# Row sums moved to the end of a PV batch, the range check moved ahead of the next inverse, and loads spread behind every second mask

## The chip, the cores and the metric

The kernel runs on one core of a Trainium2 chip. The metric is the device time of one execution in microseconds; lower is better. The same kernel is up to 2.8 us slower on one chip than on another (the kernel before: medians of 609.1 to 611.9 us), so an experiment is always told as its ratio to the kernel before on the same chip.

## The reference, cut to what matters

Two independent attention layers, A and B, with sliding-window causal masks:

```python
B, S, D = 1, 2048, 1024;  H = 32; Dh = 32; W = 256
qkv = (x @ wqkv).reshape(B, S, 3, H, Dh).transpose(2, 0, 3, 1, 4)
scores = einsum("bhqd,bhkd->bhqk", q, k) * Dh ** -0.5
mask = (i - j >= 0) & (i - j < 256)
p = softmax(where(mask, scores, -1e9))
return einsum("bhqk,bhkd->bhqd", p, v).transpose(...).reshape(B, S, D) @ wo
```

## The kernel before

The program is a list of 152 sessions. A session computes one set of score tiles on TensorE (line 511), takes exp of them on ScalarE (L521), and cuts the window out with masks on GpSimd (L532, L545). Behind some masks GpSimd clears one column of a buffer (a guard for the load that follows), and SyncE issues that load. Every second session, as a rule, ends with one or two PVs on TensorE: probabilities times values, and probabilities times ones, which gives the row sums of the softmax. The PVs of one session are called a batch. The rest of a session is filled with pieces of the projections, as "whole" 128x512 matmuls or, in sessions with a PV, as four strips of 32 columns.

```python
edgep = tile_pool(name="edge", bufs=2)          # the buffers of `both`
...
while len(pieces.get(free, [])) >= min(2 if key[0] == "x" else 4, <masks of that session>):
    free += 1                                   # the session that issues a load
...
def diag(a, g, j, i):
    nc.gpsimd.affine_select(out=diags[(g, p)]..., in_=pt..., ...)
    load_piece(now)                             # a load behind every mask, as long as there is one

def edge(g, p):                                 # VectorE: two masked parts added, so that
    both = edgep.tile([P, 4, 2, P], BF16)       # one matmul with ones can sum both (L559)
    ... tensor_tensor(out=both..., in0=dg..., in1=pts..., op=ALU.add)

def pv(g, p):
    moves = [...values..., ...sums over pt...]
    sums = edges.pop((g, p)) if p else dg
    moves += [(i, 0, 2 * P, P, sums[:, :, i, :]) for i in range(2)]     # the sums over `both`
    for x, (h, j, o, w_, src) in enumerate(moves): ...matmul...          # L592
    # norm, on VectorE: reciprocal (L605), two shuffles, multiply (L612),
    # and after every second multiply the range check of the inverses (L615):
    scalar_tensor_tensor(out=top, in0=inverses..., scalar=IN_RANGE, in1=top, xor, or)
...
    while due and due[0][0] <= now:             # end of a session: one or two PVs
        finish_norm(1)
        pv(pg, pk)
...
finish_norm()
certify[0](top)                                 # reduce the range checks
emit(END + 10, 2 * NS_MM * CT)                  # two pieces of projection meanwhile
certify[1](ps_proj)                             # verdict: TensorE sums it over partitions
```

`both` has two buffers, and a buffer comes free when the row sums over it have been computed on TensorE. All loads go through the one queue of SyncE, in the order in which they are issued. And when the program is built, the scheduler takes an x for landed three sessions after the one that issues its last piece (`arrival[key] = free + 3`), and from then on it may place projections that read it.

## Time and profile before

| | |
|---|---|
| time | 609.8 us |
| span of the profiled execution | 608.7 us |
| TensorE busy | 96% |
| VectorE, ScalarE, GpSimd busy | 67%, 68%, 59% |

The prediction below shows the lines on TensorE. The groups of the page for the engines around it are read for their last two columns: the time for which the engine sat idle just before this group, and what ended most of that.

```profile
L521 ACT ACTIVATE pt<-st 128x1024 bf16<-128x1024 f32 x304 | 302.2, 1026 | 107.9 <-PE st L511 55.1
L532 POOL TENSOR_SCALAR_AFFINE_SELECT diag<-pt 128x256 bf16<-128x256 bf16 x512 | 211.2, 438 | 195.2 <-ACT pt L521 181.7
L559 DVE TENSOR_TENSOR both<-diag,pt 128x512 bf16<-128x512 bf16 (+1 forms) x256 | 123.7, 525 | 55.5 <-PE acc L592 27.4
```

Each of them waits for another engine for a large share of the run.

### The profile page before, as it was taken

How to read it: one execution, taken by the hardware profiler on the slowest of the kernel's cores; microseconds unless marked ns; L12 is line 12 of the kernel's file. 1: busy time of each engine (PE TensorE's matmuls, PEld its weight loads, DVE VectorE, ACT ScalarE, POOL GpSimd, SP SyncE). 2: the span in 40 equal slices, each digit the busy share in tenths (PEclk: the TensorE clock that was granted, in tenths of full speed). 3: DMA queues.
4: the chain of work that ended last, by engine and by line, in shares of the span. 5: the costliest groups of instructions: out<-in, count | busy, mean ns of one | idle time of the engine just before them, and what ended most of it. 6: DMA issues, size and time to landing. Idle time of an engine off the chain costs nothing.

```text
span 608.7 us, 32535 instructions
## 1 busy us (share of the span) xinstructions
PE 586.9 (96%) x14364; PEld 363.4 (60%) x14439; DVE 409.8 (67%) x1144; ACT 412.1 (68%) x523; POOL 361.1 (59%) x918
## 2 busy tenths in 40 slices
PE   9999999999999999999999999999999999999996
PEld 6566566657655666665665766675555665555443
DVE  1388786877887867866587766766868777767200
ACT  4577867777678778786567766777667677765332
POOL 0567666767777676766466666666666666664000
PEclk9999999999999999999999999999999999999998
DMA  9714110111034102454211100112030030114222
GB/s 238 177 53 128 38 38 5 38 37 39 4 65 80 40 3 51 98 93 105 52 38 37 38 4 4 45 32 73 2 86 24 18 95 11 56 55 133 71 78 65
DMA packets 86820, 35.73 MB, mean 59 GB/s; under 512 B 65552, under 2 KB 86160, under 8 KB 86672
## 3 DMA queue, kind: packets, MB, share of 16 engines
q1 hardware_dynamic: 85632, 33.31, 22.3%
q8 instruction: 115, 1.88, 1.3%
q10 hardware_dynamic: 1040, 0.26, 0.2%
q14 instruction: 33, 0.27, 0.2%
HBM read 17.83 MB, written 8.39 MB: 43 GB/s over the span
## 4 chain that ended last, share of the span: by engine, by line
PE 65%; issue 1%; ACT 0%; DVE 0%; ACTq 0%
PE pp L197 31%; PE pp L201 19%; PE acc L592 8%; PE st L511 6%; ACT pt L521 0%; ACT osb L220 0%; DVE unsafe_i L888 0%; PE pp L887 0%; ACTq L220 0%; ACT kT L220 0%
## 5 line engine op out<-in xcount | busy, mean ns | idle before, releaser
L521 ACT ACTIVATE pt<-st 128x1024 bf16<-128x1024 f32 x304 | 302.2, 1026 | 107.9 <-PE st L511 55.1
L532 POOL TENSOR_SCALAR_AFFINE_SELECT diag<-pt 128x256 bf16<-128x256 bf16 x512 | 211.2, 438 | 195.2 <-ACT pt L521 181.7
L559 DVE TENSOR_TENSOR both<-diag,pt 128x512 bf16<-128x512 bf16 (+1 forms) x256 | 123.7, 525 | 55.5 <-PE acc L592 27.4
L545 POOL TENSOR_SCALAR_AFFINE_SELECT pt<-pt 128x512 bf16<-128x512 bf16 (+1 forms) x256 | 155.6, 626 | 0.0
L197 PE MATMUL pp<-xT,wqk 128*128 128x512 bf16 (+1 forms) x581 | 135.8, 373 | 6.5 <-issue 5.2
L605 DVE RECIPROCAL rinv<-acc 128x128 f32<-128x128 f32 x128 | 121.6, 950 | 27.2 <-PE acc L592 25.4
L201 PE MATMUL pp<-xT,wqk 128*32 128x512 bf16 x1608 | 96.9, 379 | 0.0
L197 PEld LDWEIGHTS <-wqk 128*128 128x128 bf16 x638 | 59.1, 98 | 62.3 <-issue 0.3
L197 PE MATMUL pp<-wo_sb,oT 128*128 128x512 bf16 (+1 forms) x349 | 77.7, 374 | 2.2 <-issue 1.6
L511 PEld LDWEIGHTS <-kT 32*64 32x64 bf16 x3904 | 41.7, 103 | 57.6 <-issue 56.3
L197 PE MATMUL pp<-wv,xT 128*128 128x256 bf16 x587 | 71.0, 273 | 0.3 <-issue 0.3
L511 PE MATMUL st<-qT,kT 32*64 32x64 bf16 (+4 forms) x3904 | 66.7, 236 | 1.9 <-issue 0.9
L610 DVE STREAM_SHUFFLE wide<-rinv 128x128 f32<-128x128 f32 x256 | 64.3, 296 | 0.0
L220 ACT CAST osb<-pp 128x512 bf16<-128x512 f32 (+1 forms) x61 | 35.4, 581 | 42.1 <-PE pp L197 28.7
L197 PEld LDWEIGHTS <-xT 128*128 128x128 bf16 x587 | 55.5, 98 | 11.9 <-issue 0.4
L201 PEld LDWEIGHTS <-wqk 128*32 128x32 bf16 x1608 | 42.1, 97 | 31.4 <-issue 0.2
L197 PEld LDWEIGHTS <-oT 128*128 128x128 bf16 x367 | 34.7, 98 | 39.5 <-issue 0.2
L201 PE MATMUL pp<-wv,xT 128*32 128x256 bf16 x1748 | 55.7, 273 | 2.4 <-issue 2.1
L612 DVE TENSOR_TENSOR oT<-acc,wide 128x256 bf16<-128x256 f32 x128 | 54.4, 425 | 4.4
L201 PEld LDWEIGHTS <-xT 128*32 128x32 bf16 x1748 | 46.2, 97 | 7.8 <-issue 4.1
L592 PE MATMUL acc<-pt,vt 128*32 128x128 bf16 (+2 forms) x1792 | 48.8, 223 | 0.0
L592 PEld LDWEIGHTS <-vt 128*32 128x32 bf16 x2816 | 43.5, 96 | 7.7 <-issue 0.4
(47 smaller groups left out, 385.7 us busy)
## 6 DMA issues: line engine op xcount, KB each, us to landing
out_dram<-osb SPq DMA_DIRECT2D x63, 128.0 KB, 1.9
wqk<-in_B_wqkv_dram SPq DMA_DIRECT2D x32, 128.0 KB, 2.8
wqk<-in_A_wqkv_dram SPq DMA_DIRECT2D x24, 128.0 KB, 3.0
wo_sb<-in_A_wo_dram SPq DMA_DIRECT2D x16, 128.0 KB, 2.7
wv<-in_B_wqkv_dram SPq DMA_DIRECT2D x16, 128.0 KB, 3.6
wo_sb<-in_B_wo_dram SPq DMA_DIRECT2D x16, 128.0 KB, 2.3
oT<-in_A_x_dram SPq DMA_DIRECT2D x4, 256.0 KB, 5.1
wv<-in_A_wqkv_dram SPq DMA_DIRECT2D x2, 512.0 KB, 5.7
```

The lines of the kernel that those rows point to most:

```text
L197: nc.tensor.matmul(out[:, lo:hi], lhsT=lhsT, rhs=rhs, start=start, stop=stop, skip_group_check=True)
L201: nc.tensor.matmul(out[c:c + 32, lo:hi], lhsT=lhsT[:, c:c + 32], rhs=rhs, start=start, stop=stop, tile_position=(0, c), skip_group_check=True)
L220: nc.scalar.copy(out=out, in_=in_)
L511: nc.tensor.matmul(scores[c * HALF:(c + 1) * HALF, r, a * HALF:(a + w_) * HALF], lhsT=kT[rows, keys], rhs=qT[rows, q:q + w_ * HALF], start ...
L521: nc.scalar.activation(out=pt[:, lo:lo + 2, :n * HALF], in_=scores[:, lo:lo + 2, :n * HALF], func=ACT.Exp, bias=-SHIFT, scale=cfg.scale)
L532: nc.gpsimd.affine_select(out=diags[(g, p)][:, :, h, lo:lo + HALF], in_=pt[:, :, a * HALF:(a + 1) * HALF], pattern=[[0, 4], [1, HALF]], co ...
L545: nc.gpsimd.affine_select(out=blk, in_=blk, pattern=[[0, 4], [-1, w_ * HALF]], compare_op=ALU.is_gt, fill=0.0, base=-HALF * (us[a][2] - 3) ...
L559: nc.vector.tensor_tensor(out=both[:, :, h, o:o + w_], in0=dg[:, :, h, o:o + w_], in1=pts[t][:, :, a:a + w_], op=ALU.add)
L592: nc.tensor.matmul(acc[32 * r:32 * r + 32, o:o + w_], lhsT=lhsT, rhs=src[:, r, :], start=(x == 0), stop=(x == len(moves) - 1), tile_positi ...
L605: nc.vector.reciprocal(out=inverses[0][:, turn % 2, :], in_=acc[:, 2 * P:3 * P])
L610: nc.vector.stream_shuffle(out=wide[:, h * P:(h + 1) * P], in_=inverses[0][:, turn % 2, :], mask=[16 * h] * 32)
L612: nc.vector.tensor_tensor(out=oTs[(pi, k)][:, t, (p % 2) * 256:(p % 2 + 1) * 256], in0=acc[:, 0:256], in1=wide[:], op=ALU.mult)
```

## The change

Its intent: the row sums over `both` need VectorE's additions, so they go last in a session's batch, to give VectorE time. The range check stood between a norm and the next additions, so it goes ahead of the next inverse. And the loads' guards delay GpSimd's masks, so they are spread.

```diff
-            while len(pieces.get(free, [])) >= min(2 if key[0] == "x" else 4, <masks of the session>):
+            while len(pieces.get(free, [])) >= min(3, (calls_of(free) + 1) // 2):
...
-            load_piece(now)
+            if calls.pop():                    # calls = [False, True] * 8
+                load_piece(now)
...
-        for x, (h, j, o, w_, src) in enumerate(moves):
+        def move(x): ...the same four matmuls...
+        for x in range(len(moves) - 2):
+            move(x)
+        return lambda: finish_pv(g, p, acc, [lambda x=x: move(x) for x in (-2, -1)])
...
             if turn % 2 == 0:
+                check_range()
                 inverses[0] = normp.tile([P, 2, P], F32, name="rinv")
...
-            if turn % 2:
-                nc.vector.scalar_tensor_tensor(... range check ...)
...
+        tails = []
         while due and due[0][0] <= now:
-            finish_norm(1)
-            pv(pg, pk)
+            finish_norm(0 if tails else 1)
+            tails.append(pv(pg, pk))
+        for f in tails:
+            f()
...
     finish_norm()
+    check_range()
     certify[0](top)
```

(The same lines recur for the second kind of mask and for the PVs after the last session.)

The first pair of lines holds the cap on the loads of one session. It falls from four to three for the weights, but for x it rises from two to three.

## The prediction

> **What bounds the kernel now.** I read the page from the top: shares first, then the chain that ended last.
>
> ```profile
> PE 586.9 (96%) x14364; PEld 363.4 (60%) x14439; DVE 409.8 (67%) x1144; ACT 412.1 (68%) x523; POOL 361.1 (59%) x918
> ...
> PE 65%; issue 1%; ACT 0%; DVE 0%; ACTq 0%
> PE pp L197 31%; PE pp L201 19%; PE acc L592 8%; PE st L511 6%; ACT pt L521 0%; ACT osb L220 0%; DVE unsafe_i L888 0%; PE pp L887 0%; ACTq L220 0%; ACT kT L220 0%
> ```
>
> Every other engine is idle a third of the time, and the chain is all TensorE. So only what makes TensorE run fewer columns, change shape less often, or stand still can change the time. Next I made a ledger of TensorE. The built program has 14,438 matmuls in its fast path. Starts of whole 128x512 matmuls are 216 ns apart in the trace; I charged 216 ns per 512 columns, a quarter of it for one of four column strips (128*32), an eighth for a score tile (32*64): 549 us in all. A session (152 of them: scores, exp, masks, sometimes one or two PVs, then filler projections) changes the array's shape twice. The gap that the trace shows beyond the streaming, quartile of each kind: scores to whole 146 ns, scores to PV 134, strips to scores 103, whole to scores 93. With 78, 74, 74 and 78 of them that is 36 us. Together some 586 us. The last matmul starts at 602.8 us, the first at 1.3 us; so 15 to 16 us are left, of which some 5 are the start (waiting for the first rows of x, cold clock). The remaining 10 or 11 us are stalls of TensorE in the steady state: the most that this change could win (1.7%).
>
> The waits by engine say where they are not:
>
> ```profile
> PE pp L201 <- issue: 2.1, 4, 0.9
> PE acc L592 <- DVE both L559: 0.5, 2, 0.3
> PEld L511 <- issue: 56.3, 153, 0.6
> PEld L201 <- issue: 4.7, 9, 1.2
> PEld L592 <- issue: 2.7, 10, 0.4
> ```
>
> The 56.3 us at L511 are the shape changes, once a session. What a semaphore causes looks small (0.5 us), because a wait that begins under a modelled matmul end isn't counted. So I went to the timeline. The worst PV batch:
>
> ```profile
> 82.72 0.56 DVE L615 SCALAR_TENSOR_TENSOR top<-rinv,top 128x256 int32<-128x256 int32 x1
> ...
> 83.20 2.27 DVE L559 TENSOR_TENSOR both<-diag,pt 128x512 bf16<-128x512 bf16 x4
> ...
> 83.88 0.24 PE L592 MATMUL acc<-both,ones 128*32 128x128 bf16 x4 [0.18 <-DVE both L559]
> ...
> 84.42 0.24 PE L592 MATMUL acc<-both,ones 128*32 128x128 bf16 x4 [0.30 <-DVE both L559]
> ...
> 85.19 0.57 PE L592 MATMUL acc<-both,ones 128*32 128x128 bf16 x8
> 85.40 0.94 DVE L605 RECIPROCAL rinv<-acc 128x128 f32<-128x128 f32 x1
> ```
>
> VectorE does the range check (0.56 us), then four edge additions; TensorE meets the row sums over `both` before they are there, four times. Against an unhindered batch this one lost 1.39 us. Measured so, seven batches (ending at 38, 78, 86, 125, 172, 258 and 439 us) lost 2.9 us: the first kind of stall. The second kind has no semaphore:
>
> ```profile
> 204.24 0.70 PEld L201 LDWEIGHTS <-xT 128*32 128x32 bf16 x26
> 204.29 0.93 PE L201 MATMUL pp<-wv,xT 128*32 128x256 bf16 x25
> ...
> 206.17 1.16 PE L201 MATMUL pp<-wv,xT 128*32 128x256 bf16 x35 [0.95 <-issue]
> 206.17 0.88 PEld L201 LDWEIGHTS <-xT 128*32 128x32 bf16 x34 [1.23 <-issue]
> ...
> q8 instruction: 115, 1.88, 1.3%
> ```
>
> It stops in mid-chain, where no data can be missing. Counting weight loads, these stops fall at the same place modulo 256 TensorE instructions (weight loads 4064, 5088, 5344 and on), and the 16 KB packet of the instruction queue for each had begun about 2.35 us before TensorE went on. They are instruction fetches that come too late, about 7.4 us in the whole run.
>
> **What the Trainium skill says.** "TensorEngine Tiling (Array Packing)", Key Properties: changing the tiling mode drains TensorE. The trace agrees: 93 to 146 ns each. "TensorE: Matmul & The Clock Gate", Back-to-back issue gap: a warm matmul takes N/2.4 + 2.5 ns; 216 ns for 512 columns is what the trace shows. "Runtime: NRT & Kernel Launch", Instruction fetch mechanics: instructions come in 16 KiB blocks of 256, fetched one ahead, and the cost is "mostly hidden". The trace agrees on size (115 packets, 1.88 MB) but not on hidden[...]. "Perfetto Trace Analysis", Tensor Engine Instruction: matmul ends are estimated by the profiler; hence I went by starts.
>
> **The change, part by part.**
>
> Row sums at the end. The two `both` moves of each PV (8 matmuls, 0.11 us) go behind all else of the batch. No matmul is added: acc matmuls are 4,928 in both programs. Of the batches, about 51 hold two PVs. There the sums of the first PV now come after the other moves of the second, some 0.45 us later than before; those of the second only 0.11 us later. In the batch above the waits at 83.88 and 84.42 (0.18 + 0.30 in the view, 0.8 us against the unhindered pace) would be covered, and the last additions (83.20 + 2.27 = 85.47) still come late. In the other six only the very last addition was late, by 0.1 to 0.4 us; 0.11 us of each is won. That alone is 0.45 + 6 x 0.11, about 1.1 us. The price: in a two-PV batch the first reciprocal starts 0.5 us later; its acc buffer and its `both` buffer come free as much later. VectorE is 67% busy, so mostly this is absorbed.
>
> The range check. 64 of 0.41 to 0.58 us before and after; none is removed. It leaves the place between a norm and the next edge additions, and stands ahead of the next even reciprocal. In the built VectorE stream the order norm, check, additions stood 41 times (check directly ahead of additions); after the change that is nowhere, and 33 checks stand directly behind additions, where VectorE would wait for acc anyway (27.4 + 25.4 us of idle are put down to PE acc). Twelve stand behind an evacuation and 19 between two norms, where they delay the following additions as before. So about half of the seven late batches get their additions 0.4 to 0.56 us earlier: another 0.9 us, and I count 2.0 us of 2.9 for both parts.
>
> The loads. 144 guard memsets of 0.1 us remain; they stand behind every second mask, three a session at most instead of four. In load sessions a mask comes 0.1 to 0.2 us earlier, on an engine that waits for exp (181.7 us) rather than bounds. TensorE never waits for a DMA in the steady state. I give it 0.3 us. It does shift arrivals and so what the scheduler puts where: 27 projection steps change from strips to whole form (162 TensorE rows fewer, same columns), the 6.2 us session 80 is spread over later sessions, and the second half of the last weights arrives so late that the last two PVs stand back to back. The columns are the same, and so are the shape changes within one each, so the 586 us of the ledger stay.
>
> The fetches. Since the stream is shifted, the blocks of 256 are cut elsewhere. With the durations of the ledger, 23 of 111 blocks last under 3.35 us before, lacking 12.5 us in sum, of which 7.4 were really lost. After: 25 of 110, lacking 15.5. In proportion that is 9.2 us, 1.8 more. As a third of the short blocks escaped (their packet came early), I take 1.0 us.
>
> Sum: 609.8 - 2.0 - 0.3 + 1.0 = 608.5 us.
>
> **The rivals.** First, the waits only move: later row sums delay the first norm by 0.5 us, hence the next edge additions (their two buffers wait for these same row sums), and the next batch meets them late. For it: in the batches at 78, 125 and 172 us VectorE ran without a pause from the norm to the additions. Against it: those began behind an evacuation, not behind acc. It would leave 2.9 us of stalls as they are, or add one: about 610 to 611. Second, fetch decides: the recut stream stalls the full 1.8 us or more, or with luck 2 less; 607 to 611. Third, all goes well: batches wait for nothing, mask stream and loads run smoother, fewer strips ease the fetch: 5 us off, 604 to 605. Fourth, a load lands late and a projection waits on its DMA: several us at once, 613 or more. Against it: loads take 2 to 4 us to land, and the scheduler allows two or three sessions of 3.6 us.
>
> **Range and chances.** Most weight lies on a change under 0.7%. Winning 2% means 12.2 us, more than all steady stalls; losing 2% needs a new wait of 12 us, which only the fourth rival could make. I predict 608.5 us, 8 in 10 between 604.5 and 611.5; faster by over 2% 0.02, within 2% 0.955, slower 0.025.
>
> **What would show it.** TensorE busy stays within 1% of 586.9 us and the shares of the chain as they are. In PV batches the `both` matmuls stand last, eight or sixteen in a row, and stalls ahead of them sum to about 1 us. L615's successor stands ahead of reciprocals, mostly in former idle time before them. Stalls without a releaser remain at about 8 to 9 us, each behind a 16 KB packet. I am wrong if waits on VectorE's additions stay near 2.9 us, if fetch stalls fall, or if a DMA appears among the things that TensorE waits for.

## The result, and the profile after

The changed kernel took 619.2 us (619.0 to 620.5, four runs) against 609.8 us (609.7 to 610.2, four runs). The ratio is 1.0158, with a 95% interval of 1.014 to 1.0176: 9.4 us slower by the medians, well inside 2% but outside the predicted range, whose upper end was 611.5. Ratios here are the mean time of one kernel's fast runs over that of the other's of the same rounds, so they are not quite the ratio of the medians quoted. All outputs are right. From here on L numbers of the changed kernel are shifted: scores L514, `both` L566, PV L607, norm L631 to L638, check L573.

From the page of the changed kernel, the shares and the chain that ended last:

```profile
PE 588.3 (95%) x14281; PEld 363.2 (59%) x14358; DVE 402.4 (65%) x1136; ACT 417.4 (67%) x531; POOL 361.0 (58%) x918
...
PE 86%; DVE 6%; issue 4%; POOL 2%; ACT 0%; POOLq 0%; DVEq 0%; ACTq 0%
```

TensorE's work is the same (588.3 against 586.9 us). The span is 10.1 us longer, so TensorE stands still longer. The chain says in what: VectorE, GpSimd and "issue" now hold parts of it. The waits of TensorE in the changed kernel (columns: total us, times, longest us):

```profile
PE pp L201 <- issue: 5.6, 9, 1.7
PE acc L607 <- DVE both L566: 2.0, 4, 0.5
PE pp L197 <- POOL xT L396: 1.6, 1, 1.6
...
PE pp L913 <- DVE okp L908: 1.2, 1, 1.2
PE pp L197 <- POOL pt L551: 0.9, 1, 0.9
```

Before, the first two were 2.1 and 0.5 us, and the other three are not in the list. The weight loads tell the first of them from their own side; 4.7 us became

```profile
PEld L201 <- issue: 8.6, 10, 1.9
```

and VectorE's wait for a free buffer, 27.4 us in 16 waits before, became

```profile
DVE both L566 <- PE acc L607: 50.2, 24, 4.0
```

Since waits under a modelled matmul end are counted too short, I also took the ledger of the prediction and subtracted, for every weight load in the two traces, the ledger's time of its matmul from its start. That lag of TensorE behind its ledger only grows. I sorted each step of its growth by where it stands: within a few instructions of a boundary of 256 instructions ("fetch"), in PV batches, at a projection whose x had not landed, at the verdict, and the rest (mostly many steps of 0.15 us at shape changes). In us:

| | start | fetch | PV | x late | verdict | rest | sum |
|---|---|---|---|---|---|---|---|
| before | 2.3 | 5.4 | 1.3 | 0 | 0 | 5.7 | 14.7 |
| after | 3.1 | 8.8 | 2.6 | 2.1 | 1.2 | 7.3 | 25.1 |

The sums differ by 10.4 us and the spans by 10.1, so the table accounts for the loss. It is my own count from the traces and the built programs, and stands in no view. The profiled execution of the changed kernel was the slowest of its four (620.5 us). A single step can be put in the wrong column where two causes coincide.

### The profile page after: what moved, and what is told of

Same layout as the page of the kernel before. It is cut to its first block, busy times and chain, and to the rows that moved or that the text cites. A ratio compares the mean times of both kernels' runs of the same rounds, so it can differ in the third digit from the quotient of the medians.

```text
span 618.8 us, 32372 instructions
## 1 busy us (share of the span) xinstructions
PE 588.3 (95%) x14281; PEld 363.2 (59%) x14358; DVE 402.4 (65%) x1136; ACT 417.4 (67%) x531; POOL 361.0 (58%) x918
## 4 chain that ended last, share of the span: by engine, by line
PE 86%; DVE 6%; issue 4%; POOL 2%; ACT 0%; POOLq 0%; DVEq 0%; ACTq 0%
PE pp L197 42%; PE pp L201 24%; PE acc L607 11%; PE st L514 8%; DVE rinv L631 2%; DVE both L566 2%; POOL diag L535 1%; DVE wide L636 1%; PE pp L675 1%; DVE oT L638 1%; POOL pt L551 1%; DVE top L573 0%; PE acc L689 0%; DVE kT L222 0%; ACT pt L524 0%
## 5 line engine op out<-in xcount | busy, mean ns | idle before, releaser
L566 DVE TENSOR_TENSOR both<-diag,pt 128x512 bf16<-128x512 bf16 (+1 forms) x256 | 116.1, 492 | 73.2 <-PE acc L607 50.2
L197 PE MATMUL pp<-xT,wqk 128*128 128x512 bf16 (+1 forms) x605 | 141.6, 373 | 9.5 <-issue 5.7
L631 DVE RECIPROCAL rinv<-acc 128x128 f32<-128x128 f32 x128 | 121.9, 953 | 28.1 <-PE acc L607 24.4
L197 PEld LDWEIGHTS <-wqk 128*128 128x128 bf16 x664 | 61.3, 98 | 68.3 <-issue 2.3
L201 PE MATMUL pp<-xT,wqk 128*32 128x512 bf16 x1504 | 90.9, 379 | 0.4 <-issue 0.4
L514 PEld LDWEIGHTS <-kT 32*64 32x64 bf16 x3904 | 41.7, 103 | 57.5 <-issue 56.3
L514 PE MATMUL st<-qT,kT 32*64 32x64 bf16 (+4 forms) x3904 | 66.8, 236 | 2.3 <-issue 1.5
L638 DVE TENSOR_TENSOR oT<-acc,wide 128x256 bf16<-128x256 f32 x128 | 54.4, 425 | 4.4
L201 PEld LDWEIGHTS <-wqk 128*32 128x32 bf16 x1504 | 39.1, 97 | 30.7 <-issue 0.9
L607 PE MATMUL acc<-pt,vt 128*32 128x128 bf16 (+2 forms) x1792 | 48.8, 223 | 0.0
L607 PEld LDWEIGHTS <-vt 128*32 128x32 bf16 x2816 | 43.4, 97 | 7.5 <-issue 0.4
```

The source lines that it names most:

```text
L197: nc.tensor.matmul(out[:, lo:hi], lhsT=lhsT, rhs=rhs, start=start, stop=stop, skip_group_check=True)
L201: nc.tensor.matmul(out[c:c + 32, lo:hi], lhsT=lhsT[:, c:c + 32], rhs=rhs, start=start, stop=stop, tile_position=(0, c), skip_group_check=True)
L514: nc.tensor.matmul(scores[c * HALF:(c + 1) * HALF, r, a * HALF:(a + w_) * HALF], lhsT=kT[rows, keys], rhs=qT[rows, q:q + w_ * HALF], start ...
L566: nc.vector.tensor_tensor(out=both[:, :, h, o:o + w_], in0=dg[:, :, h, o:o + w_], in1=pts[t][:, :, a:a + w_], op=ALU.add)
L607: nc.tensor.matmul(acc[32 * r:32 * r + 32, o:o + w_], lhsT=lhsT, rhs=src[:, r, :], start=(x == 0), stop=(x == -1), tile_position=(0, 32 * ...
L631: nc.vector.reciprocal(out=inverses[0][:, turn % 2, :], in_=acc[:, 2 * P:3 * P])
```

## The experiments

The theory after this reading: three new waits (PV, x, verdict), which the three parts of the change made, and over 3 us of fetch stalls because the shifted stream is cut elsewhere. The rival: the fetch stalls are a by-product of the slower flow and not of where the cuts fall, and the parts of the change cost all of it.

### Each part alone

Each of the three parts was put alone into the kernel before; the edits are the parts of the diff above.

**Row sums alone.**

> The kernel before with the row sums of a PV batch at its end, nothing else of the change. The TensorE stream keeps its 28,905 instructions and its cuts into blocks of 256. Theory A (the loss is instruction fetch, late x loads and the verdict at the end, all brought by the loads part): within 1.5 us of before, 608.5 to 610.5. Rival B (later row sums delay norms and edge additions, batches wait): 3 us or more above before, with the waits of acc matmuls on both rising from 0.5 us to several.

Measured: ratio 1.0031 (1.0013 to 1.005), that is 1.9 us slower: between the two forecasts. Two places show how. First the batch that the prediction had chosen as the worst. It now runs so on TensorE:

```profile
83.90 0.23 PE L594 MATMUL acc<-both,ones 128*32 128x128 bf16 x4
84.35 0.24 PE L594 MATMUL acc<-both,ones 128*32 128x128 bf16 x4 [0.22 <-DVE both L559]
85.12 0.57 PE L594 MATMUL acc<-both,ones 128*32 128x128 bf16 x8 [0.53 <-DVE both L559]
85.51 1.25 PE L201 MATMUL pp<-wv,xT 128*32 128x256 bf16 x37
```

All the other matmuls of the two PVs are now ahead of these, as intended. But VectorE's four additions still run from 83.13 to 85.40, and the last sums must wait for them. From the start of the batch to the first projection behind it are 2.51 us (83.00 to 85.51); before they were 2.51 us too (83.07 to 85.58). Two covered waits turned into one longer one, because the last addition sets the end. Second, a new late batch, seen in VectorE's timeline of the kernel before,

```profile
111.66 1.11 DVE L559 TENSOR_TENSOR both<-diag,pt 128x512 bf16<-128x512 bf16 x2 [2.02 <-POOL wqk L393]
...
116.85 1.44 DVE L559 TENSOR_TENSOR both<-diag,pt 128x256 bf16<-128x256 bf16 x3
```

and in that of the row sums alone:

```profile
112.39 1.29 DVE L559 TENSOR_TENSOR both<-diag,pt 128x512 bf16<-128x512 bf16 x2 [2.47 <-PE acc L594]
...
117.87 1.67 DVE L559 TENSOR_TENSOR both<-diag,pt 128x256 bf16<-128x256 bf16 x3
```

The first addition now waits for a PV matmul, the later row sums, to free its buffer. Two norms stand behind it in VectorE's order without a pause, and so the additions for the next batch begin 1.0 us later, at 117.87 (TensorE's own part of this batch begins 0.3 us later). TensorE gets to those sums at 118.5 and stands until 119.6.

**Range check alone.**

> The kernel before with the range check moved ahead of the next even reciprocal, nothing else. Theory A: within 1 us of before (608.8 to 610.5), except that the verdict at the end may cost up to 0.5 us. Rival B (VectorE order matters): 2 us or more either way.

Measured: 0.9999 (0.9981 to 1.0016), nothing. TensorE's waits for `both`, as the profile counts them, did not fall but rose from 0.5 to 1.3 us, and in the lag the PV column rose from 1.3 to 1.7 us while the fetch column fell from 5.4 to 4.4. In the batch near 84 us the check did leave its place ahead of the additions, but TensorE reached this batch earlier against VectorE's norms: the additions began 0.27 us after its first matmul (0.13 before), and it took 2.49 us instead of 2.51.

**Loads alone.**

> The kernel before with the loads behind every second mask and at most three a session, nothing else. The TensorE stream becomes that of the changed kernel (28,740 instructions; blocks of 256 that last under 3.35 us lack 15.5 us in sum instead of 12.5). Theory A: nearly the whole loss is here, 616.5 to 619.5, with two waits of TensorE on x transposes near sessions 72 and 80 and the verdict late at the end. Rival B: 611 or less, since only the row sums make it slow.

Measured: 1.0108 (1.008 to 1.0136), 6.6 us slower (615.0 us), the largest of the three, though less than the "nearly the whole loss" that was expected. In the lag: fetch 6.8 (+1.4), a late x 1.1, the verdict 1.2, the rest +1.6 us. The wait at the verdict (1.2 us) is there with this part alone and with neither of the others: the last weights of the output projection arrive later, and so the scheduler puts the last two PVs back to back.

The three ratios add to 1.0138 of 1.0158, but this should not be read as proof that the parts explain it all. The loads part also shifts the instructions. The two other parts don't: their streams keep their length, and with the check alone TensorE's stream is that of the kernel before, matmul for matmul.

### Moving the boundaries without touching the work

In the warm-up at the very start, whole matmuls on a blank tile are split into strips. This adds weight-load and matmul pairs while TensorE waits for x anyway, and shifts every later instruction against the boundaries of 256.

```diff
 def keep_warm(n):
     for _ in range(n):
-        nc.tensor.matmul(warm[:], lhsT=blank[:, 0:P], rhs=blank[:, 0:512], ...)
+        # m = 16, 8, 4 or 1: m strips with together the columns of one whole matmul
+        for i in range(m): nc.tensor.matmul(warm[c:c + 32, o:o + w_], ..., tile_position=(0, c))
```

The changed kernel, 62 pairs or 124 instructions more:

> The changed kernel whole, but eight and more of the warm-up matmuls at the start are made of four or eight column strips of the same columns: 124 TensorE instructions more before the first session, so that all later blocks of 256 are cut elsewhere. By the durations of the ledger the short blocks now lack 6.4 us in sum instead of 15.5. Theory A: the fetch stalls fall from about 12 us to about 5, so the time falls by 5 to 8 us, to 611 to 614. Rivals (PV waits or late loads make the loss): 618.5 to 620, unchanged.

Measured: 1.0028 (1.0011 to 1.0045). Of 9.4 us, some 8 are gone, without a change to any sum, check or load. The stalls in mid-chain shrank from 8.6 us in the changed kernel to

```profile
PEld L201 <- issue: 2.0, 3, 0.8
```

and the fetch column of the lag from 8.8 to 2.2 us.

The kernel before, 132 instructions more:

> The kernel before with 132 more TensorE instructions among the warm-up matmuls (same columns), so that its blocks of 256 are cut elsewhere; its short blocks then lack 8.2 us in sum instead of 12.5. Fetch theory: some 2.5 to 3.5 us faster than before, 605.5 to 607.5. Rival (the gain of the shifted changed kernel came from the warm-up itself, a hotter clock or an earlier start): a gain of the same 8 to 9 us here too, or none.

Measured: 1.005 (1.0027 to 1.0073): slower instead of faster. The expectation failed. The tally of short blocks that the prediction used (how much the blocks lack of 3.35 us) had promised less fetch, but the fetch column went from 5.4 to 6.0 us. Where boundaries fall matters, but this tally does not say how. Nor are the 3 us all fetch: TensorE's waits for `both` doubled as well, from 0.5 to 1.0 us as the profile counts them. A shift moves other waits with it.

In the text of the next run, "62 matmuls earlier" should read 31: the shift is 31 pairs or 62 instructions. In the text for all repairs, further down, the shift by 124 moves the boundaries by 124 instructions and not by "248".

The changed kernel, 62 more:

> The changed kernel with 62 more matrix instructions in the warm-up, half the shift that took 8.8 us away. If only where the fetch boundaries fall decides, this is a third draw from the same urn: the tally of short blocks is 13.3 us (15.5 unshifted, 6.4 shifted by 124), so by the tally 616 to 619 us; if the shift by 124 helped for another reason (the longer warm-up), the time falls by about half as much, to 614 to 615 us. The trace must show the stalls at the new boundaries, 62 matmuls earlier in the program than in the changed kernel.

Measured: 1.0046 (1.0016 to 1.0077). Fetch 5.3 us, and no late x. The tally had said 616 to 619 us; 612.8 was measured.

The kernel before, 62 more:

> The kernel before with 62 more matrix instructions in the warm-up; the tally of short blocks hardly moves (12.5 to 12.7 us). The shift by 132 cost 3 us where the tally promised a gain of as much, so I expect only a scatter of some 4 us: 608 to 614 us, ratio 0.997 to 1.007. Near 1.000 says that the kernel before has no special luck with its boundaries; over 1.005 again says that it had.

Measured: 0.9974 (0.9954 to 0.9995). Fetch 3.2 us. Here a shift alone makes the unchanged kernel 1.6 us faster.

By then it could still be that a longer warm-up helped by itself. A shift by exactly 256 decides that: it has the longest warm-up of all, but every boundary is back at the same instruction.

The changed kernel, 256 more:

> The changed kernel with 256 more instructions (128 pairs of weight load and matmul) in the warm-up: every later instruction keeps its place within a 256-instruction block. If the place of the fetch boundaries decides: 617 to 621 us, ratio 1.011 to 1.019, with the stalls of the changed kernel at the same instructions again (near 170, 250, 348, 388 and 500 us). If more strips in the warm-up help by themselves: 608 to 611 us, as the shift by 124 did.

Measured: 1.0126 (1.0101 to 1.0151): most of the loss is back (7.7 of 9.6 us). The weight loads of one of the stalls, first in the changed kernel and then in the one shifted by 256:

```profile
385.91 0.86 PEld L201 LDWEIGHTS <-xT 128*32 128x32 bf16 x29
388.70 0.33 PEld L201 LDWEIGHTS <-xT 128*32 128x32 bf16 x14 [1.94 <-issue]
389.25 0.30 PEld L514 LDWEIGHTS <-kT 32*64 32x64 bf16 x28 [0.21 <-issue]
```

```profile
383.40 1.62 PEld L201 LDWEIGHTS <-xT 128*32 128x32 bf16 x55
386.12 0.33 PEld L201 LDWEIGHTS <-xT 128*32 128x32 bf16 x14 [1.10 <-issue]
386.67 0.30 PEld L514 LDWEIGHTS <-kT 32*64 32x64 bf16 x28 [0.21 <-issue]
```

It is the same stop, 14 weight loads before the next session's scores, with no data missing: 1.94 and 1.10 us. The other stalls came back too, at weight loads 4062, 6238, 8664, 8920 and 12502 of the one and exactly 128 weight loads later in the other.

The kernel before, 256 more:

> The kernel before with 256 more instructions in the warm-up, every boundary where it was: ratio 0.998 to 1.002 if the boundaries decide. If more strips help by themselves: 0.990 to 0.997.

Measured: 1.002 (0.9997 to 1.0043), no better than the kernel before. So the longer warm-up does not help. The place of the boundaries decides, with all that hangs on it.

The changed kernel, 186 more:

> The changed kernel with 186 more instructions, a fourth place of the boundary (after 0, 62 and 124); the tally of short blocks is 10.1 us, between 6.4 and 13.3, so 610 to 615 us if the tally orders the changed kernels as it has so far (15.5: 619.2; 13.3: 612.8; 6.4: 610.5).

Measured: 1.0104 (1.008 to 1.0128), a miss of the expected 610 to 615 us: 616.1. Fetch is 5.2 us, but x is late by 2.5 us.

The kernel before, 186 more:

> The kernel before with 186 more instructions (places 0, 62 and 132 gave 1.000, 0.997 and 1.005). I expect 608 to 613 us, ratio 0.996 to 1.005. The mean of the four places is then about 1.000 for the kernel before, against about 1.006 for the changed one: the change itself would cost some 3 to 4 us and the place of its boundaries the other 6.

Measured: 1.0023 (1.0001 to 1.0046). Fetch 5.4 us.

Counted in the built programs of the changed kernel and its four shifts, every stop of over 0.4 us after the start, outside PVs, late x and verdict, stands at the same place: at TensorE instruction 191 or 192 modulo 256, whatever work the shift has put there.

Now both kernels have four places of the boundary, about a quarter of a block apart (for the changed kernel at 124 the mean of two runs, the second of which is told below):

| shift | 0 | 62 | 124 (before: 132) | 186 | mean |
|---|---|---|---|---|---|
| before, ratio | 1 | 0.9974 | 1.0050 | 1.0023 | 1.0012 |
| before, fetch us | 5.4 | 3.2 | 6.0 | 5.4 | 5.0 |
| after, ratio | 1.0158 | 1.0046 | 1.0015 | 1.0104 | 1.0081 |
| after, fetch us | 8.8 | 5.3 | 2.5 | 5.2 | 5.5 |

On average the changed kernel is 0.7% or about 4 us slower, and its fetch stalls are then almost those of the kernel before. With four places that scatter by 0.6% this mean is uncertain by some 2 us. The 9.4 us of the measured pair is this cost and a bad draw of the boundaries, of which fetch alone is 3.3 us (8.8 against its mean of 5.5; the kernel before, with 5.4 against 5.0, is near its own).

### The three new waits, one at a time

**A third buffer for `both`**, in the kernel with the row sums alone:

```diff
-    edgep = ctx.enter_context(tc.tile_pool(name="edge", bufs=2))
+    edgep = ctx.enter_context(tc.tile_pool(name="edge", bufs=3))
```

> Row sums at the end of a batch alone, with three buffers for the summed edges instead of two. If the part costs time because edge additions wait for a buffer that the late row sums still read: the wait of VectorE's additions on acc matmuls falls from 42.6 us to under 15, TensorE's on the additions from 1.8 us to under 0.5, and the time comes to that of before or 1 us under it. If it costs time because the first norm of a batch starts later: 1 to 2 us above before as with two buffers.

Measured: 1.0004 (0.9982 to 1.0026), where the row sums with two buffers were 1.0031. The chips differ and the two intervals overlap, so the times alone do not show a gain; the traces show where it is. The waits of VectorE for a buffer are gone from its list, and TensorE's for `both` fell from 1.8 to 0.7 us (expected: under 0.5); at the place shown above VectorE reads

```profile
112.05 0.64 DVE L559 TENSOR_TENSOR both<-diag,pt 128x512 bf16<-128x512 bf16 x1 [0.31 <-POOL wqk L393]
...
116.68 1.45 DVE L559 TENSOR_TENSOR both<-diag,pt 128x256 bf16<-128x256 bf16 x3
```

and the batch at 119 us is not late any more. The PV column is 1.2 us, as in the kernel before. So what the row sums cost in this trace was the buffer, and without that cost no gain of theirs can be measured.

**The same buffer with the check alone.**

> The kernel before with the range check moved ahead of the next inverse, and three buffers for the edge sums. The check alone cut the waits of the PV batches for the edge sums from 2.9 us to 1.3 us and the time by nothing that could be measured; the third buffer cut them in the row-sums kernel from 1.8 to 0.7 us. If these waits are on the path, 0.5 to 1.5 us faster than before, ratio 0.9975 to 0.999; if the fetch takes back what they give, 1.000 to 1.002.

Measured: 0.9998 (0.9983 to 1.0012). The hoped for 0.5 to 1.5 us did not come. (The "2.9 us to 1.3 us" of that text compares two ways of counting; in the profile's own the check alone had raised these waits.) The batches at 84 and 125 us are still late, at 2.42 and 1.67 us against 2.51 and 1.21 in the kernel before: VectorE comes to their additions straight from its norms, so they are late by its work and not for want of a buffer.

**More work between the two steps of the verdict**, in the changed kernel. Its end reads, first on VectorE and then on TensorE:

```profile
571.14 0.95 DVE L631 RECIPROCAL rinv<-acc 128x128 f32<-128x128 f32 x1
...
573.01 0.41 DVE L573 SCALAR_TENSOR_TENSOR top<-rinv,top 128x256 int32<-128x256 int32 x1
...
574.24 0.15 DVE L908 TENSOR_SCALAR okp<-pm 128x1 f32<-128x1 f32 x1
```

```profile
569.70 3.63 PE L197 MATMUL pp<-wo_sb,oT 128*128 128x512 bf16 x15
574.54 0.19 PE L913 MATMUL pp<-okp,ones 128*1 128x1 f32 x2 [1.21 <-DVE okp L908]
```

VectorE has the norms of two PVs, the last check and the reduction to do one after the other, and the two pieces of projection that TensorE was given are over 1.2 us too early.

```diff
-    emit(END + 10, 2 * NS_MM * CT)
+    emit(END + 10, 6 * NS_MM * CT)
```

> The changed kernel with 48 instead of 16 projection steps between the last range check on VectorE and the small matmul that reads its verdict. If TensorE really waits there: 1.0 to 1.4 us faster than the changed kernel, 617.5 to 618.5, and no wait of TensorE on okp. If that wait was hidden anyway: 619 to 619.6.

Measured: 1.0124 (1.0102 to 1.0145), and the wait is gone from the trace. 1.0158 less 1.0124 is 2.1 us, but on another chip, and the two intervals touch; the wait itself was 1.2.

**The late x.** The wait at 259.9 us is for the second quarter of B's x, which eight transposes bring. SyncE's queue in the kernel before, and then in the changed one:

```profile
240.37 14.42 SPq L158 DMA_TRANSPOSE xT<-in_B_x_dram  x8
```

```profile
244.78 13.80 SPq L158 DMA_TRANSPOSE xT<-in_B_x_dram  x8
```

They start 4.4 us later. But the whole program is late by then: the scores of the session in which these loads begin start at 237.3 us before and at 240.8 after. Counted from there, the last of the eight lands after 19.1 us (at 256.4) in the kernel before and after 19.3 us (at 260.1) in the changed one, so against the program x is hardly later. What moved is TensorE's first use of it. In the kernel before it is

```profile
258.37 2.56 PE L201 MATMUL pp<-xT,wqk 128*32 128x512 bf16 x44
```

and in the changed one

```profile
257.92 0.42 PE L514 MATMUL st<-qT,kT 32*64 32x192 bf16 x20
259.91 2.32 PE L197 MATMUL pp<-xT,wqk 128*128 128x512 bf16 x9 [1.57 <-POOL xT L396]
```

Counting the groups of scores, the first is in session 72 (of 0 to 151) and the second in session 71, although the program runs later. With three x loads a session instead of two, the guards of the eight stand in three sessions instead of four; so the scheduler takes this x for landed one session earlier, and places its projection there. The transfers became no faster. The third and last quarters moved likewise, from session 77 to 76 and from 80 to 79, and the last is waited for at 290 and 291 us. That the raised cap is the cause is read from the programs and traces; no run with a cap of two for x alone tested it.

The releaser named is a guard of GpSimd. In the built program this weight load also waits for four of the queues that carry x, and the last piece that it needs landed at 259.71. The run that was meant to test this issued loads of x one session earlier:

```diff
+            if key == ("x", 1, 0):
+                ahead.setdefault(free - 1, []).append((new, where, f))
```

> The changed kernel with the eight transposing loads of the first block of the second x one session earlier; the order of all TensorE instructions is the same. If TensorE waits for that load at 258 to 260 us: 1.0 to 1.6 us faster than the changed kernel, 617.5 to 618.5, and that wait is gone. If the load was only blamed: 619 to 620.

Measured: 1.0156 (1.0131 to 1.0182), nothing. But the edit moved the wrong loads. The key `("x", 1, 0)` is the first quarter of B's x, whose eight transposes begin at 181.8 us in the changed kernel and now at 175.6:

```profile
181.83 11.66 SPq L158 DMA_TRANSPOSE xT<-in_B_x_dram  x8
```

```profile
175.63 1.22 SPq L158 DMA_TRANSPOSE xT<-in_B_x_dram  x1
```

TensorE first reads that quarter at about 245 us, so it was never late. The late quarter kept its place and its wait (0.85 us at 258 and 1.46 us at 290). This run says nothing about the late x. Nor is this wait in every changed kernel: 2.1 us of late x unshifted, none with the shift by 62, 0.4 and 1.1 by 124, 2.5 by 186, 1.1 by 256. The eight transposes take 11.3 us in one run and 13.8 in another. So it is a margin that the change used up, and then a matter of luck.

### All repairs together

The changed kernel with the shift by 124, the third buffer, the longer verdict, and the loads of `("x", 1, 0)` six sessions earlier (beside the diffs above for buffer, verdict and warm-up). This last one is again the first quarter of B's x, not the late one: its transposes begin at 156.9 us, and the late quarter stays behind its weight loads.

```diff
+            if key == ("x", 1, 0):
+                ahead.append((free - 6, (new, where, f)))
+                pieces.setdefault(free, []).append(None)     # its old place stays counted
...
     def load_piece(now):
+        early = ahead.pop(0)[1] if ahead and ahead[0][0] <= now else None
```

> The changed kernel with four repairs: 124 more matrix instructions in the warm-up (strips for whole matmuls, same work), which move every fetch boundary by 248 instructions; six rather than two pieces of projection between the two steps of the verdict; three buffers for the edge sums rather than two; and the eight loads of the first half-block of B's input put into the queue ahead of two groups of weight loads. If the loss is the sum of fetch (8.8 us of lag, 2.2 with this shift), edge sums (2.6 to about 1), the late load (2.1 to under 1) and the verdict (1.2 to 0), the time is 606 to 609 us, ratio 0.994 to 1.000. If the four only hide one another, it stays at the 610.5 us (1.003) of the shift alone.

Measured: 0.996 (0.9947 to 0.9973), 608.8 us against 611.2 of the kernel before. The fetch column is 3.4 us, PV 1.2, x 0.9, the verdict 0. The late x is no smaller than with the shift alone (0.4 and 1.1), as it must be, since its loads were not moved.

The shift alone and all repairs were then run beside each other on one chip, since their ratios had come from two. The shift alone:

> The changed kernel with 124 more instructions at its start, as run before (1.0028 of the kernel before on another chip). If ratios carry over from chip to chip, 1.001 to 1.005 again; if the chip's own fetch latency moves them, as much as 0.998 to 1.003.

With the repairs:

> The same with the three repairs, beside it on one chip. If the repairs take what the verdict (1.2 us), the row sums (1.2 us) and some of the other waits cost, it is 2.0 to 4.5 us faster than the shifted changed kernel, ratio to the kernel before 0.994 to 0.999. If the profiled spans were right, 0.5 to 1.5 us.

Measured: 1.0002 (0.9986 to 1.0018) and 0.9943 (0.9926 to 0.9959), medians of 611.9 and 608.3 us, the kernel before 611.9. The three edits together, buffer, verdict and the moved first quarter, are worth 3.6 us at the same place of the boundary; they were not taken apart here. That agrees with the 4 us of the four-place mean. It also shows how far a ratio carries: the same shifted kernel was 1.0028 on one chip and 1.0002 on another, with intervals that just overlap. The repaired version beats the kernel before by 0.4 to 0.6%, but its place of the boundary is a good one (3.4 to 3.9 us of fetch against 5.4), so only a part of that is due to the change.

## Why the prediction was wrong

**The bound: right.** TensorE's work is the same to 1.4 us, and everything that happened was a matter of TensorE standing still. "Losing 2% needs a new wait of 12 us" was the frame in which 9.4 us did happen.

**"I count 2.0 us of 2.9 for both parts": wrong.** Row sums and check are worth +1.9 and 0 us alone. The step that failed is that a covered wait was counted as won: in the worst batch "the waits at 83.88 and 84.42 ... would be covered". They were, and the batch is as long as before (2.51 us), because the last addition sets its end. The batch at 125 us tells the same: 1.21 us from its first matmul to the projection behind it, before (123.87 to 125.08) and with the row sums moved (125.11 to 126.32). The price that the same paragraph mentioned and dismissed ("VectorE is 67% busy, so mostly this is absorbed") was the real effect: the `both` buffers come free later, VectorE's wait for them went from 27.4 to 50.2 us, and next batches met late additions. This is the first rival, and the trace with the third buffer, in which that wait and the late batch are gone, shows it. Its estimate of one more microsecond was about right: the PV column rose by 1.3 us.

**"The loads. I give it 0.3 us": wrong in sign, and the largest of the parts (6.6 us alone, boundaries included).** The step that failed is the reading of the change as "three a session at most instead of four". For x it is three instead of two, and so the scheduler put the first projections of three quarters of x one session earlier, while the transfers landed no sooner against the program; two of the three were waited for. "TensorE never waits for a DMA in the steady state" was true of the kernel before. The fourth rival (a load lands late) was put aside because "loads take 2 to 4 us to land, and the scheduler allows two or three sessions of 3.6 us". That is the time of one load; here the first of eight was issued at 244.78 us, and the last landed at 260.1, 15.3 us later. The rival happened at 259.9 and 291 us, with 2.1 us rather than the "several" that it said. The prediction also saw that "the last two PVs stand back to back", and did not follow it to the end: it is a chain of two norms, a check and a reduction against two pieces of projection, and it left TensorE waiting 1.2 us.

**"The fetches ... I take 1.0 us": the mechanism right, the size wrong.** The fetch column rose by 3.4 us. That the cuts decide is shown: a shift by 124 takes 6.6 us of fetch and 8 us of time away, and a shift by 256 brings most of it back. But the tally of short blocks failed as a measure in the kernel before, where a tally reduced from 12.5 to 8.2 us went with a slower kernel, and missed the changed one at a shift of 62. Since a shift of either kernel moves the time by several microseconds, a range of 7 us in all (604.5 to 611.5) was too narrow: the measured ratios of the four places of the changed kernel reach from 1.0015 to 1.0158.

**In sum:** instead of -2.0 - 0.3 + 1.0, the lag reads PV +1.3, late x +2.1, verdict +1.2, fetch +3.4, start +0.8 and rest +1.6 us, 10.4 in all. The start differs from run to run (1.8 to 3.1 us over all traces). About 4 us are the change itself, by two estimates: the repairs on one chip (3.6 us) and the mean over boundary places, which is uncertain by 2 us. The others are where this program's boundaries fall, and what follows from it. Open is the rest: many small steps at shape changes, which no run took apart, how fetch and late x feed each other (in the shift by 62 both fell at once), and what the late x alone costs, since no run repaired it.

## What to carry to other kernels

Moving a consumer later within a batch wins only if the last producer is not what ends the batch, and it holds the producer's buffer longer: look at who waits for that buffer, or give it one more, before you move it. When a repair changes nothing, check in the trace that it moved the instruction that was late. Before changing how many loads a session may issue, ask when the last of each group lands and when the scheduler will believe that it has, and follow the last instructions of the program through to the end. In this kernel, one long unrolled stream bound by TensorE, where the instruction blocks are cut moved the time by 0.8% (before) and 1.4% (after) from best to worst: in one like it, try several shifts of both kernels before a difference of that size is put down to the change.

## What the Trainium skill lacked or had wrong

- "Runtime: NRT & Kernel Launch", Instruction fetch mechanics, calls the crossing of a 16 KiB boundary "mostly hidden". In these traces it costs TensorE 2.2 to 8.8 us of a run of 610 us, with single stops up to 1.9 us, and a shift of the stream by 124 instructions changes the time by 8 us.
- The same section gives TensorE an instruction memory of 128 KiB, 2048 instructions. If all of it were filled ahead, one would expect a single short block not to matter; but the stops stand at boundaries of 256, and come back at the same instructions when the stream is shifted by 256 (ratios of 1.0126 and 1.0158 with the boundaries there, 1.0002 to 1.0104 with a shift by 62, 124 or 186).
- I found no page that says how much the time of the same transposing loads scatters: eight of them, in the same place of the changed kernel's queue, took 11.3 to 13.8 us over its shifts (a part of it may be waiting for guards).
- I found no page that says how far a ratio of two kernels carries from chip to chip: the same kernel read 1.0028 on one and 1.0002 on another, and the kernel before 609.1 to 611.9 us.
